# Attention feeding a mixture of experts: value products with the score tile stationary, and rows turned by DMA

## The chip, the cores and the metric

The kernel runs on one core of a Trainium2 chip. The metric is device time in microseconds (us), lower is better. The core has a matrix engine (TensorE, PE in the tables, with its weight loads as PEld), VectorE (DVE), ScalarE (ACT), GpSimd (POOL), and SyncE (SP), whose queue issues most DMAs. TensorE reads a stationary operand (loaded by LDWEIGHTS) and streams a moving one past it; results go to PSUM, eight banks of 128 x 512 f32.

## What is computed

```python
# u, v: (8, 2496, 256)   z: (8, 2496, 64)   w1: (8, 256, 1024)   w2: (8, 1024, 256)
scores = (1.0 / S) * z @ z.T                 # per batch, S = 2496
attn   = np.maximum(scores, 0.0) ** 2
x      = (u * (attn @ v)).reshape(B * S, D)  # D = 256
xn     = x / (norm(x) + 1e-6)                # rows
logits = xn @ en.T / tau                     # en: 8 normalized expert rows
e      = argmax(logits)                      # one expert per token
out    = softmax(logits)[e] * (relu(x @ w1[e]) @ w2[e])
```

All in f32 accuracy. The kernel gets it from f16 matmuls: an operand is scaled by a power of two and split into a high and a low f16 half, and a product is the sum of high x high, low x high and high x low.

## The kernel before

**Stages.** First attention for all 8 batches with routing of each finished group of tokens to a table of rows in DRAM (`xs`, sorted by expert), then the expert stage: slots of 256 or 128 rows of one expert, `slot_up` and `slot_down`.

**Attention.** A batch has 2496 tokens: 5 groups of query tokens (four of 512, the last of 448), and 20 tiles of 128 keys (the last of 64). A step is one key tile `s` against one group `g`, so 100 steps a batch, 800 in all. `scores` (two matmuls, L232 and L233) makes a tile of 128 keys x 512 tokens in PSUM, ScalarE applies relu and square (L235, L236), and `parts` splits it on VectorE into high and low half (`hl`, L242 and L243, five buffers). The score matrix is symmetric, so only 60 of the 100 steps of a batch compute their tile ("own" steps: `s // 4 >= g`); the other 40 read a tile that was turned by a DMA transpose (L250, tile `tt`) when its mirror was made. `LOOK = 3` makes scores three own steps ahead and halves two ahead.

**Value products.** `values` (L261 to L274) holds a 128 x 128 piece of v (`va` high, `vb` low) stationary and moves the score tile, 512 columns, past it. Its result is 128 columns of v by 512 tokens, two accumulators (`acc`, two of three PSUM banks of pool `psA`) for the 256 columns. In the last step of a group both halves of the 64 keys share a tile (`twin`), so it has four matmuls for six.

**Routing.** When a group is done, `route` returns a list of pieces; one is taken per step of the next group. `gate_x` (L302) multiplies by u, still with tokens along the columns. For each of the four blocks of 128 tokens, `turn` (L308, L309) multiplies the block in f32 by an identity with the expert rows beside it, which gives the rows by token and the logits in one PSUM bank (`pm`, one buffer), and `take` copies them out (L326 on ScalarE, L327 on VectorE). Then the norm (`root`, `scale`), the split of the row into f16 halves (L351, L352), the choice of the expert, its place by a small matmul (`rank`, L399, L400), and four indirect DMAs on POOL (L424) that write the rows (`row`, two buffers) to `xs`.

**Start and look-ahead.** v's scale needs its maximum. For every batch it is read once for that (`scan`, eight loads of 312 KB into two buffers, L104, L110) and once more tile by tile for the products (`vt`, L198). For the next batch, `ahead` spreads these pieces over the steps of the current one; weights of the experts are split along the way (`weights`).

**Order.** A scheduler places the instructions on each engine's queue; every engine then works through its queue in order.

## Time and profile before

| | |
|---|---|
| median of three runs | 2256.31 us (2252.34 to 2259.57) |
| the profiled execution | 2257.18 us |
| its span in the trace | 2255.4 us |
| PE busy | 2177.3 us, 97% |
| DVE busy | 1422.9 us, 63% |
| ACT busy | 1095.7 us, 49% |
| DMA queue 1 (SP), share of 16 engines | 50.8% |

A busy share says how long an engine had an instruction in it; ends of matmuls are modelled, so two starts in a row tell more than a length. A row of the waits says which engine waited for whom, in total, how often, and the longest.

### The profile page before, as it was taken

To read this page: it belongs to the slowest core of one execution; us is meant where nothing else is said; L and a number is where in the kernel's file an instruction comes from. 1 tells how busy PE (TensorE), PEld (TensorE's weight loads), DVE (VectorE), ACT (ScalarE), POOL (GpSimd) and SP (SyncE) were. 2 spreads that over 40 slices of the span, in tenths; PEclk is the share of its full clock that TensorE was granted. 3 is DMA by queue.
4 is the path that set the end of the run, shared out by engine and by line. 5 is a ranking of instruction groups with operands and counts; after the bars stand their busy time and mean duration, and the time that the engine had idled before them with its cause. 6 is when DMAs were issued, how large, how long until landed. Compare 5 with 4: busy or idle time off the path is not lost. (4 is left out here: it accounts for less than half of the span.)

```text
span 2255.4 us, 42995 instructions
## 1 busy us (share of the span) xinstructions
PE 2177.3 (97%) x14922; PEld 1430.6 (63%) x14922; DVE 1422.9 (63%) x4339; ACT 1095.7 (49%) x2201; POOL 354.2 (16%) x432
## 2 busy tenths in 40 slices
PE   6999999999999999999999999999999999999987
PEld 2444445445445444445445458888888888888886
DVE  7888879788788788888788655333333333333332
ACT  6667667667568577667666642222222222222221
POOL 0011111111111111111111112111111111111211
PEclk8999999999999999999999999999999999999998
DMA  7947766765947858776655535333123223167453
GB/s 186 231 105 211 166 165 145 190 148 136 229 102 192 190 118 199 155 181 144 155 140 112 101 93 147 74 86 94 48 72 109 48 74 107 51 181 218 120 137 108
DMA packets 528267, 308.30 MB, mean 137 GB/s; under 512 B 446885, under 2 KB 489390, under 8 KB 519856
## 3 DMA queue, kind: packets, MB, share of 16 engines
q1 hardware_dynamic: 512672, 264.31, 50.8%
q0 software_dynamic: 15376, 41.24, 5.0%
q8 instruction: 117, 1.92, 0.4%
q14 instruction: 102, 0.84, 0.1%
HBM read 287.91 MB, written 60.12 MB: 154 GB/s over the span
## 5 line engine op out<-in xcount | busy, mean ns | idle before, releaser
L235 ACT ACTIVATE a<-sc 128x512 f32<-128x512 f32 (+1 forms) x480 | 282.8, 589 | 169.7 <-PE sc L233 125.3
L236 ACT ACTIVATE a<-a 128x512 f32<-128x512 f32 (+1 forms) x480 | 299.8, 625 | 13.3
L836 POOL DMA_INDIRECT out_dram<-ot,me x163 | 158.6, 973 | 696.9 <-DVE ot L835 422.3
L274 PEld LDWEIGHTS <-vv 128*128 128x128 f16 x1520 | 149.0, 98 | 179.2 <-issue 8.8
L273 PEld LDWEIGHTS <-vv 128*128 128x128 f16 x1520 | 149.1, 98 | 173.6 <-issue 17.8
L272 PEld LDWEIGHTS <-vv 128*128 128x128 f16 x1520 | 149.0, 98 | 161.8 <-ACT vv L217 2.3
L424 POOL DMA_INDIRECT xs<-row,dsti x160 | 171.3, 1071 | 499.4 <-DMA xs<-row,dsti 336.3
L272 PE MATMUL acc<-tt,vv 128*128 128x512 f16 (+1 forms) x640 | 236.4, 369 | 9.4 <-DVE xt L302 9.3
L274 PE MATMUL acc<-tt,vv 128*128 128x512 f16 (+1 forms) x640 | 236.2, 369 | 0.0
L273 PE MATMUL acc<-tt,vv 128*128 128x512 f16 (+1 forms) x640 | 236.2, 369 | 0.0
L232 PE MATMUL sc<-z 128*128 128x512 f16 (+1 forms) x480 | 183.7, 383 | 10.7 <-DVE z L189 10.7
L233 PE MATMUL sc<-z,z 128*128 128x512 f16 (+1 forms) x480 | 183.8, 383 | 0.0
L829 PE MATMUL po<-w,hh 128*128 128x256 f16 x648 | 177.4, 274 | 3.1 <-DMA w<-wsd 3.1
L829 PE MATMUL po<-wb,hh 128*128 128x256 f16 x656 | 178.9, 273 | 0.0
L830 PE MATMUL po<-wb,hh 128*128 128x256 f16 x656 | 178.8, 273 | 0.0
L831 PE MATMUL po<-wb,hl 128*128 128x256 f16 x656 | 178.8, 273 | 0.0
L831 PE MATMUL po<-w,hl 128*128 128x256 f16 x648 | 177.4, 274 | 0.0
L830 PE MATMUL po<-w,hh 128*128 128x256 f16 x648 | 177.4, 274 | 0.0
L805 PEld LDWEIGHTS <-wa 128*128 128x128 f16 x1472 | 145.3, 99 | 30.2 <-DMA wa<-wsd 16.8
L806 PEld LDWEIGHTS <-wa 128*128 128x128 f16 x1472 | 145.4, 99 | 13.3
L807 PEld LDWEIGHTS <-wa 128*128 128x128 f16 x1472 | 145.4, 99 | 13.1
L835 DVE TENSOR_SCALAR ot<-po,me,w 128x256 f32<-128x256 f32 x81 | 40.8, 540 | 157.2 <-PE po L831 155.9
(4216 smaller groups left out, 5165.2 us busy)
## 6 DMA issues: line engine op xcount, KB each, us to landing
wa<-wsd SPq DMA_DIRECT2D x92, 1024.0 KB
wb<-wsd SPq DMA_DIRECT2D x46, 1026.0 KB
w<-wsd SPq DMA_DIRECT2D x46, 1026.0 KB
scan<-in_v_dram SPq DMA_DIRECT2D x64, 312.0 KB
vt<-in_v_dram SPq DMA_DIRECT2D x152, 128.0 KB
ut<-in_uT_dram SPq DMA_DIRECT2D x32, 512.0 KB
wr<-in_w_dram SPq DMA_DIRECT2D x16, 1024.0 KB
wsd<-wo SPq DMA_DIRECT2D x16, 1024.0 KB
```

What stands on the lines that cost most here:

```text
L232: nc.tensor.matmul(sc[:, :n], z1[:, ss], z1[:, t0:t0 + n], start=True, stop=False)
L233: nc.tensor.matmul(sc[:, :n], z1[:, ss], z2[:, t0:t0 + n], start=False, stop=True)
L235: state["at"] = nc.scalar.activation(a[:, :n], sc[:, :n], AF.Relu, scale=2.0 ** -SHIFT).ins
L236: nc.scalar.activation(a[:, :n], a[:, :n], AF.Square)
L272: nc.tensor.matmul(acc[k][:, :n], va, ph[:, :n], start=first, stop=False)
L273: nc.tensor.matmul(acc[k][:, :n], va, pl[:, :n], start=False, stop=False)
L274: nc.tensor.matmul(acc[k][:, :n], vb, ph[:, :n], start=False, stop=last)
L424: nc.gpsimd.indirect_dma_start(xs[:, :], bass.IndirectOffsetOnAxis(ap=loc["dsti"][:m, j:j + 1], axis=0), row[:m, j, :], None)
L829: nc.tensor.matmul(o, hh[:, f, t], wh, start=(f == 0), stop=False)
L830: nc.tensor.matmul(o, hh[:, f, t], wl, start=False, stop=False)
L831: nc.tensor.matmul(o, hl[:, f, t], wh, start=False, stop=(f == NF - 1))
L836: nc.gpsimd.indirect_dma_start(out, bass.IndirectOffsetOnAxis(ap=me.bitcast(U32)[:, j, 1:2], axis=0), ot[:, j, :], None, bounds_check=N - ...
```

## The change

Values: the stationary operand is a 128 x 128 piece of the score tile (128 keys by 128 tokens, one half), the moving operand is v's high or low half, 256 columns; an accumulator bank holds two blocks of 128 tokens by 256 columns. A pair of banks holds the group's four blocks. In the 448-token group, the 64 odd tokens' high and low halves stand side by side (`apart`, `both`), so one load serves both. Turned tiles of that group are laid out to match, and the last key tile is turned in two DMAs.

Routing: `gate_x` writes rows by token at once; `turn` and the old `take` are gone. ScalarE makes the high half of the row (it was VectorE's), `flips` turns the f16 row by four DMA transposes on SP's queue, and three empty pieces later `logits` multiplies the turned halves by the split expert rows (`enr`), 16 small matmuls for a group, which one `take` reads. `row` has three buffers; u is read by token and its tile has one buffer; PSUM: three banks for scores, four for accumulators.

Start and look-ahead: the first batch's v is loaded once in five loads, kept in buffers of the turned tiles, and reduced there; for later batches the scan pieces begin at step 4 and stand four steps apart, each reduction eight steps after its load.

```diff
-    psS = ctx.enter_context(tc.tile_pool(name="psS", bufs=4, space=PSUM))
-    psA = ctx.enter_context(tc.tile_pool(name="psA", bufs=3, space=PSUM))
+    psS = ctx.enter_context(tc.tile_pool(name="psS", bufs=3, space=PSUM))
+    psA = ctx.enter_context(tc.tile_pool(name="psA", bufs=4, space=PSUM))
...
+    def first_load(c0):
+        if c0 % VB == 0:
+            first[c0 // VB] = tp.tile([P, VB, D], F32, name="vall", tag="tt")
+        t = first[c0 // VB]
+        j = c0 % VB
+        m = min(VC, NST - c0)
+        full = min(m, S // P - c0)
+        if full:
+            nc.sync.dma_start(t[:, j:j + full, :], v[0, c0 * P:(c0 + full) * P, :].rearrange("(j p) d -> p j d", p=P))
...
         n = groups[g][1]
-        vv = Vs[b, s]
-        first, last = s == 0, s == NST - 1
-        for k in ks:
-            va = vv[:, k * P:(k + 1) * P]
-            vb = vv[:, D + k * P:D + (k + 1) * P]
+        va, vb = Vs[b, s][:, 0:D], Vs[b, s][:, D:]
+        last = s == NST - 1
+        for j in range(ceil_div(n, P)):
+            m = min(P, n - j * P)
+            o = acc[j // 2][:, (j % 2) * D:(j % 2 + 1) * D]
+            first = s == 0 and j % 2 == 0
+            ph, pl, both = hl(j)
             if twin and last:
-                nc.tensor.matmul(acc[k][:, :n], va, ph[:, :n], start=first, stop=False)
-                nc.tensor.matmul(acc[k][:, :n], vb, pl[:, :n], start=False, stop=True)
-                continue
-            nc.tensor.matmul(acc[k][:, :n], va, ph[:, :n], start=first, stop=False)
-            nc.tensor.matmul(acc[k][:, :n], va, pl[:, :n], start=False, stop=False)
-            nc.tensor.matmul(acc[k][:, :n], vb, ph[:, :n], start=False, stop=last)
+                todo = [(o[:m], ph, va), (o[:m], pl, vb)]
+            elif both is not None:
+
+                todo = [(o, both, va), (o[:m], ph, vb)]
+            else:
+                todo = [(o[:m], ph, va), (o[:m], ph, vb), (o[:m], pl, va)]
+            for k, (dst, w, x) in enumerate(todo):
+                nc.tensor.matmul(dst, w, x, start=first and k == 0, stop=last and k == len(todo) - 1,
+                                 skip_group_check=True)
...
-        row = rt.tile([P, 4, ROW], F32, name="row", tag="row")
+        row = rt.tile([P, 4, ROW], F32, name="row", tag="row", bufs=3)
...
         def gate_x():
             for k in range(2):
-                nc.vector.tensor_tensor(xt[:, k, :n], acc[k][:, :n], ut[:, k, :n], op=ALU.mult)
-
-        def turn(j):
-            def f():
-                pm = psM.tile([P, 512], F32, name="pm", tag="m")
-                c = slice(j * P, (j + 1) * P)
-                nc.tensor.matmul(pm[:, 0:P + E], xt[:, 0, c], rhs0, start=True, stop=False, skip_group_check=True)
-                nc.tensor.matmul(pm[:, P:2 * P + E], xt[:, 1, c], rhs1, start=False, stop=True, skip_group_check=True)
-                loc["pm"] = pm
-                state["pm"] = True
-                if j:
-                    square(j - 1)
-            return f
+                m = min(2, full - 2 * k)
+                if m > 0:
+                    nc.vector.tensor_tensor(x[:, 2 * k:2 * k + m, :], acc[k].rearrange("p (j d) -> p j d", d=D)[:, :m, :],
+                                            ut[:, 2 * k:2 * k + m, :], op=ALU.mult)
+            if rem:
+                o = acc[full // 2][:, (full % 2) * D:(full % 2 + 1) * D]
+                if apart(g):
+                    t = rt.tile([P, D], F32, name="tl", tag="sq", bufs=1)
+                    nc.scalar.copy(t[:rem], o[rem:])
+                    nc.vector.tensor_tensor(t[:rem], o[:rem], t[:rem], op=ALU.add)
+                    o = t
+                nc.vector.tensor_tensor(x[:rem, full, :], o[:rem], ut[:rem, full, :], op=ALU.mult)
...
         def split(j):
             up = loc["up"][:, j:j + 1]
-            nc.vector.tensor_scalar_mul(row16[:, j, 0:D], x[:, j, :], up)
+            nc.scalar.activation(row16[:, j, 0:D], x[:, j, :], AF.Copy, scale=up)
             nc.vector.scalar_tensor_tensor(row16[:, j, D:2 * D], x[:, j, :], up, row16[:, j, 0:D],
                                            op0=ALU.mult, op1=ALU.subtract)
 
@@ -357,6 +432,32 @@
                 for j in range(j0, min(j0 + 2, nj)):
                     split(j)
             return f
+
+        def flips(j0):
+
+            def f():
+                for j in range(j0, min(j0 + 2, nj)):
+                    nc.sync.dma_start_transpose(xt[:, j], row16[:, j, 0:2 * D])
+            return f
+
+        def logits():
+            pm = psM.tile([P, 512], F32, name="pm", tag="m")
+            for j in range(nj):
+                for c in range(4):
+                    w = 2 * E if c < 2 else E
+                    nc.tensor.matmul(pm[:, 2 * E * j:2 * E * j + w], xt[:, j, c, :], enr[:, c % 2, 0:w],
+                                     start=(j == 0 and c == 0), stop=(j == nj - 1 and c == 3), skip_group_check=True)
+            loc["pm"] = pm
+            state["pm"] = True
+
+        def take():
+            pv = loc.pop("pm")[:, 0:2 * E * nj].rearrange("p (j a e) -> p j a e", a=2, e=E)
+            state["pm"] = False
+            lo = rt.tile([P, 4, E], F32, name="lo", tag="lo")
+            nc.vector.tensor_copy(lo[:, :nj, :], pv[:, :, 1, :])
+            nc.vector.tensor_tensor(lg[:, :nj, :], pv[:, :, 0, :], lo[:, :nj, :], op=ALU.add)
+            nc.vector.tensor_tensor(lg[:, :nj, :], lg[:, :nj, :],
+                                    loc["inv"][:, :nj].unsqueeze(2).broadcast_to([P, nj, E]), op=ALU.mult)
...
+        wait = lambda: None
+        return [gate_x, squares(0), squares(2), root, scale, splits(0), splits(2), flips(0), flips(2), wait, wait, wait,
+                logits, take, top, exps, rank, gates, place, scatters]
...
@@ -870,15 +964,15 @@
     def ahead(b):
 
         todo = []
-        at = min(NST + 4, NB // 4)
+        at = min(4, NB // 16)
         for i, what in enumerate(SCANS):
-            todo.append((at + 2 * i, False, lambda w=what: scan_load(b + 1, *w)))
-            todo.append((at + 2 * i + 4, False, lambda w=what: scan_max(b + 1, *w)))
-        at += 2 * len(SCANS) + 4
+            todo.append((at + 4 * i, False, lambda w=what: scan_load(b + 1, *w)))
+            todo.append((at + 4 * i + 8, False, lambda w=what: scan_max(b + 1, *w)))
+        at += 4 * len(SCANS) + 8
         for k, what in enumerate("zv"):
             for j, f in enumerate(scale_pieces(b + 1, what)):
-                todo.append((at + 8 * k + 4 * j, True, f))
```

What the scheduler makes of it shows at three places. TensorE, in the second group of the second batch, where the first group is being routed (`acc` are accumulators, `tt` and `hl` score tiles, `vv` v's halves, `pm` the routing bank). Before:

```order
L274 LDWEIGHTS vv
L274 MATMUL acc_2901<-tt,vv 128x512
L308 MATMUL pm<-rhs_234,xt 128x136
L309 MATMUL pm<-rhs_235,xt 128x136
L232 LDWEIGHTS z_322
L232 MATMUL sc<-z_322 128x512
L233 LDWEIGHTS z_322
L233 MATMUL sc<-z_323,z_322 128x512
L272 LDWEIGHTS vv
L272 MATMUL acc_2900<-hl__2873,vv 128x512
```

and now:

```order
L350 LDWEIGHTS hl__3831
L350 MATMUL acc_3583<-vv,hl__3831 128x256
L448 LDWEIGHTS xt
L448 MATMUL pm<-enr,xt 128x16
L448 LDWEIGHTS xt
L448 MATMUL pm<-enr,xt 128x16
L448 LDWEIGHTS xt
L448 MATMUL pm<-enr,xt 128x8
L448 LDWEIGHTS xt
L448 MATMUL pm<-enr,xt 128x8
```

The two f32 matmuls of a turn, which stood at four places of a group, are gone; 16 small ones (four of them here) stand at one place; and a value matmul loads a score tile and moves 256 columns of `vv`.

SP's queue, from the end of the first group of the second batch into the second (`ut` is u, `scan` a piece for the maximum of the next batch, `xt` the turned row). Before:

```order
L250 DMA_TRANSPOSE tt<-hl__2798 128x8x128
L250 DMA_TRANSPOSE tt<-hl__2820 128x8x128
L250 DMA_TRANSPOSE tt<-hl__2843 128x8x64
L281 DMA ut<-in_uT_dram 128x2x512
L250 DMA_TRANSPOSE tt<-hl__2997 128x8x128
L104 DMA scan<-in_v_dram 128x624
L250 DMA_TRANSPOSE tt<-hl__3019 128x8x128
L250 DMA_TRANSPOSE tt<-hl__3041 128x8x128
L104 DMA scan<-in_v_dram 128x624
L250 DMA_TRANSPOSE tt<-hl__3059 128x8x128
```

and now:

```order
L295 DMA_TRANSPOSE tt<-hl__3492 128x8x128
L292 DMA_TRANSPOSE tt<-hl__3528 128x4x64 x2
L105 DMA scan<-in_v_dram 128x624
L359 DMA ut<-in_u_dram 128x4x256
L105 DMA scan<-in_v_dram 128x624
L440 DMA_TRANSPOSE xt<-row 128x4x128 x4
L295 DMA_TRANSPOSE tt<-hl__3759 128x8x128
L105 DMA scan<-in_v_dram 128x624
L295 DMA_TRANSPOSE tt<-hl__3784 128x8x128
L295 DMA_TRANSPOSE tt<-hl__3809 128x8x128
```

The four flips stand in front of the second group's first turns of score tiles, behind the load of u.

VectorE at the start, around the reductions for v's maximum (`smxv`, now `smxf`; `z` are split z tiles). Before:

```order
L589 TENSOR_SCALAR eh<-en2c 8x1
L188 SCALAR_TENSOR_TENSOR z_104<-zt,scz,z_103 64x256
L591 TENSOR_SCALAR ey<-eh 8x1
L189 SCALAR_TENSOR_TENSOR z_103<-zt,scz,z_104 64x256
L594 TENSOR_TENSOR et<-ey 8x1
L242 CAST hl__377<-a 128x512
L596 SCALAR_TENSOR_TENSOR et_263<-et,en2c 8x1
L392 TENSOR_SCALAR row<-iot 128x4
L243 TENSOR_TENSOR hl__377<-a,hl__377 128x512
L110 TENSOR_REDUCE smxv<-scan 128x1
L598 SCALAR_TENSOR_TENSOR ey<-et_263,ey 8x1
L122 TENSOR_REDUCE smv<-smxv 128x1
```

and now:

```order
L234 TENSOR_REDUCE smxf<-vall 128x1 x2
L189 SCALAR_TENSOR_TENSOR z_104<-zt,scz,z_103 64x256
L276 CAST hl__174<-a 128x512
L234 TENSOR_REDUCE smxf<-vall 128x1
L284 TENSOR_TENSOR hl__174<-a,hl__174 128x512
L276 CAST hl__177<-a 128x512
L234 TENSOR_REDUCE smxf<-vall 128x1
L284 TENSOR_TENSOR hl__177<-a,hl__177 128x512
L190 SCALAR_TENSOR_TENSOR z_103<-zt,scz,z_104 64x256
L123 TENSOR_REDUCE smv<-smxf 128x1
```

The last of the reductions stands 27 places further ahead in VectorE's queue than it did.

## Rows read from the trace of the kernel before

**Rows 1.** the page, busy time of each engine, share of the span:

```profile
PE 2177.3 (97%) x14922; PEld 1430.6 (63%) x14922; DVE 1422.9 (63%) x4339; ACT 1095.7 (49%) x2201; POOL 354.2 (16%) x432
```

**Rows 2.** stretches: us, busy of each engine, clock, DMA share, GB/s:

```profile
10.00:15.00 5.00, 3.22 (x8) 1.27 (x9) 4.77 (x10) 3.15 (x7) 0.00 (x0) 1.00 0.74 226
199.53:235.74 36.21, 36.21 (x181) 17.80 (x180) 29.95 (x95) 27.68 (x54) 4.55 (x6) 1.00 0.76 143
304.94:341.38 36.44, 33.77 (x162) 16.49 (x162) 27.53 (x95) 22.61 (x52) 4.53 (x7) 0.95 0.70 190
704.54:740.04 35.50, 35.50 (x178) 17.50 (x177) 30.91 (x97) 28.87 (x58) 5.16 (x6) 1.00 0.97 218
1600.00:1800.00 200.00, 200.00 (x1835) 179.25 (x1833) 71.47 (x114) 45.38 (x76) 36.96 (x38) 1.00 0.28 73
```

**Rows 3.** TensorE in order of time: start, modelled length, line, matmul:

```profile
711.29 0.40 PE L308 MATMUL pm<-rhs,xt 128*128 128x136 f32 x2
...
711.75 0.38 PE L232 MATMUL sc<-z 128*128 128x512 f16 x1
...
715.20 0.40 PE L308 MATMUL pm<-rhs,xt 128*128 128x136 f32 x2
...
1360.27 0.27 PE L805 MATMUL ph__17140<-xt,wa 128*128 128x256 f16 x1
```

**Rows 4.** the page, costliest groups: a weight load of the value products:

```profile
L274 PEld LDWEIGHTS <-vv 128*128 128x128 f16 x1520 | 149.0, 98 | 179.2 <-issue 8.8
```

**Rows 5.** waits of TensorE, 70 to 1360 us: total, times, longest:

```profile
PE acc L272 <- DVE xt L302: 9.3, 14, 1.6
PE pm L308 <- DVE lg L327: 8.4, 10, 2.2
```

**Rows 6.** the page, costliest groups: a matmul of the down projection:

```profile
L830 PE MATMUL po<-wb,hh 128*128 128x256 f16 x656 | 178.8, 273 | 0.0
```

**Rows 7.** TensorE in order of time: rank matmuls, and 128 columns:

```profile
99.05 0.26 PE L399 MATMUL pm<-ob,ones_b 128*128 128x40 bf16 x4
...
99.18 0.38 PE L232 MATMUL sc<-z 128*128 128x512 f16 x1
...
2150.41 0.22 PE L805 MATMUL ph__30475<-xt,wa 128*128 128x128 f16 x1
2150.47 0.22 PE L806 MATMUL ph__30475<-xt,wa 128*128 128x128 f16 x1
```

**Rows 8.** VectorE, then TensorE in order of time, around a late row:

```profile
326.93 0.17 DVE L392 TENSOR_SCALAR row<-iot 128x4 int32<-128x4 f32 x1 [4.30 <-DMA xs<-row,dsti]
...
330.23 0.38 PE L272 MATMUL acc<-hl__4009,vv 128*128 128x512 f16 x1 [1.81 <-DVE hl__4009 L242]
```

**Rows 9.** VectorE and ScalarE by line, 300 to 1300 us: busy, mean ns:

```profile
L352 DVE SCALAR_TENSOR_TENSOR row<-x,up,row 128x256 f16<-128x256 f32 x120 | 56.9, 475 | 0.0
L351 DVE TENSOR_SCALAR row<-x,up 128x256 f16<-128x256 f32 x120 | 41.1, 345 | 0.0
L327 DVE COPY lg<-pm 128x8 f32<-128x8 f32 x120 | 19.4, 161 | 72.5 <-ACT x L326 72.1
...
L217 ACT ACTIVATE vv<-vt,scv 128x256 f16<-128x256 f32 x114 | 55.2, 502 | 16.3 <-PE acc L274 13.3 <-issue 0.9 <-DMA vt<-in_v_dram 0.7
L326 ACT COPY x<-pm 128x256 f32<-128x256 f32 x120 | 43.9, 366 | 114.9 <-PE pm L309 107.8 <-issue 7.0
```

**Rows 10.** a turn on SP (ns); DMA queue 1 from 208 to 232:

```profile
L250 SPq DMA_TRANSPOSE tt<-hl__2524 x1: 1237/1237/1237, 206.7 to 206.7; - x1
...
q1 hardware_dynamic: 13097, 3.26, 79.8%
```

**Rows 11.** the start: VectorE, TensorE in order of time; a ScalarE wait:

```profile
25.54 0.78 DVE L110 TENSOR_REDUCE smxv<-scan 128x1 f32<-128x624 f32 x1
...
30.32 0.63 PE L272 MATMUL acc<-hl__191,vv 128*128 128x512 f16 x1
...
ACT vv L217 <- DMA vt<-in_v_dram: 3.0, 4, 1.2
```

155 lines of the change are left out of this document (95 added, 60 removed).

## The prediction

> **What bounds the kernel now.** I read the busy table first: TensorE is busy 97% of the span, the next engine 63% [rows 1]. A busy TensorE is modelled, so I then read starts. In the table by stretches, attention (as 704 to 740) and experts (1600 to 1800) both run at a granted clock of 1.00 [rows 2]. In attention every matmul of 512 columns starts 0.2156 us after the one before: 16 from 711.75 to 715.20 [rows 3]; for 448 columns I take 0.189, in proportion. So attention is a chain of matmuls on TensorE, and the reader can add it up from counts. A batch has 100 steps, each with six value matmuls (four in the last step of a group; 4560 of the loads are on three lines with x1520 [rows 4]). That is 3776 value matmuls of 512 columns and 944 of 448: 3776 x 0.2156 + 944 x 0.189 = 992.5 us. The 60 own steps of a batch have two score matmuls each, 56 x 16 x 0.2156 + 4 x 16 x 0.189 = 205, unchanged. The expert stage, from 1360.27 on [rows 3], is unchanged too.
>
> What is not arithmetic in attention is small: waits. The list of waits from 70 to 1360 names two at its head: the accumulators wait for the gating product L302 (14 times, 9.3 us), and a turn matmul L308 waits for the logits copy L327 (10 times, 8.4 us) [rows 5].
>
> **The change, part by part.**
>
> *Value products.* The stationary operand becomes a 128x128 piece of the score tile and the moving one v's 256 columns. A full step has 12 matmuls of 256 columns for six of 512, so the columns stay; the count doubles. In the last group of a batch (448 tokens) a step has 9 + 2, because the 64 odd tokens share one load for high and low half. Total 32 x (19 x 12 + 8) + 8 x (19 x 11 + 8) = 9288. What one costs with a load of its own shows in the expert stage, where both projections move 256 columns [rows 6]: 1835 matmuls and 1833 loads in 200 us, 0.109 apart [rows 2]. 9288 x 0.109 = 1012.4, so **+19.9 us**. A load is 98 ns long [rows 4] and lies under the matmul before it; the cover is 109 ns, so it is nearly used up.
> The Trainium skill ("TensorE: Matmul & The Clock Gate", Part 3, The mechanism) says that a weight load overlaps running matmuls only when it goes to another row group. Here all use the whole array. By that rule the trace's down projection could not run at 0.109; it does. What the rule would give is a rival below.
>
> *Turns.* Rows by token need no turning, so 160 pairs of f32 matmuls go. A pair takes 711.29 to 711.75, 0.46 us [rows 3]: **-73.6 us**, all on TensorE.
>
> *Logits.* 16 small matmuls for each of 40 groups, each with its own load of 128 columns. No row shows 8 or 16 columns. Nearest are the rank matmuls, 40 columns with a load each: five between 99.05 and 99.18, 0.025 apart [rows 7]; the other end is 128 columns at 0.056 [rows 7]. I take the rank rows, which are nearer: 640 x 0.025 = **+16.0** (up to 35.8).
>
> *Waits that lose their cause.* With four accumulator banks for two groups, the next group no longer waits for L302; with one read of the logits bank per group instead of four, the waits at L308 go. Their listed 17.7 us count from a modelled end, 0.38 after a start where the spacing is 0.216, so each of 24 hides 0.16 more: **-21.5**. The third row buffer takes away a stall that starts on VectorE: at 326.93 it had stood 4.30 us for the scatter that frees a row, and TensorE then waited 1.81 (with the hidden part 2.0) for a score tile [rows 8]. Its group, 305 to 341, ran at a mean clock of 0.95 [rows 2], 1.8 of 36.4 us lost. Together **-3.8**. Of the four score banks one goes to the accumulators: nothing, since a score tile is read by ScalarE three steps before its bank is needed again.
>
> *Waits that may come.* VectorE loses the scaling L351 and the copies L327 (41.1 and 19.4 us in 300 to 1300 [rows 9]) and gets two small reads of the logits bank per group; ScalarE loses the copy L326 (43.9) and gets the scaling, by the nearest row L217 0.50 each, 60 us for the same 120 [rows 9]. Neither becomes the bound. u's tile has one buffer now, so its load waits for the gating product on SP, in front of the flips, which need that product anyway: nothing. The rows are now turned by DMA, four per group, on SP's queue. A turn of a score tile costs SP 1.24 us to issue [rows 10]; for half the bytes I take the same, since no row is smaller. Four cost 4.9 us per group, and the odd 64 tokens split one turn into two. Queued behind them on SP are the turns of the score tiles, and for those waits VectorE, which needs one of five score buffers back. On the DMA engines, 208 to 232 is nearly all such turns: 3.26 MB at 79.8%, 170 GB/s [rows 10], so a flip of 131 KB is 0.77 us, 3.1 per group. The first group of a batch, 199.53 to 235.74, stands at 0.76 (27.5 of 36.2 us [rows 2]) and would hold, with flips and four scans moved into it (312 KB at 226 GB/s over a share of 0.74, 1.0 us each [rows 2]), about 35 of 35 us. That is full; but 704 to 740 ran at 0.97 with TensorE without a gap [rows 2]. The logits stand four steps (5 us or more) behind the last flip, which covers the landing in most groups. Bounds 0 and 40 us; I take **+8**, near the row at 0.97.
> The Trainium skill ("Advanced Engine Details and Errata", X-Bar Transpose (TRN2)) calls such turns as fast as ordinary DMA, 350 to 400 GB/s. The row says 170; by the page a flip would be 0.35 us (an estimate) and this overload would not exist.
>
> *Start.* v's maximum is read with two buffers, so eight loads follow VectorE's pace, the last reduction starts at 25.54 and the first value matmul at 30.32 [rows 11]. Now five loads go out at once behind the first z loads, and stay for the products. 2.56 MB at 226 GB/s [rows 2] is 11.3 us, less than half of the time to the last reduction, so data comes several us earlier; but VectorE is busy 4.77 of 5 us there [rows 2] and its work before the first split is nearly the same. After it, ScalarE waited 3.0 us for v tiles in the first group [rows 11]; those are now there. Between 0 and 12; I take **-7**.
>
> **Sum**, against the profiled execution's 2257.2 (span 2255.4, 1.8 outside; 0.9 over the median of the three runs): +19.9 - 73.6 + 16.0 - 21.5 - 3.8 + 8 - 7 = -62.0, that is 2195.2, or **2195 us**.
>
> **Rivals.**
> *Only the arithmetic comes.* The waits are replaced by as many at the flips or in the full first groups, logits cost 0.056, the start gives nothing: 2257.2 + 19.9 - 73.6 + 35.8 = 2239. For it: the schedule before was planned as well and still had these waits; the DMA share. Against: fewer hand-overs between engines per group. 2215 to 2245.
> *Slower: SP's queue.* In the first two groups of a batch SP reaches the first flip before the split row is written and stands there; score turns queue behind it, the five buffers run out, VectorE's next cast waits and TensorE with it. Price per group: about 24 small VectorE steps of 0.16 (as L327) and four splits of 0.475 [rows 9], 5.7 us, plus 4.9 us of issue, less three buffers at 1.74 us a step (2 x 0.2156 + 12 x 0.109): 5.4. Sixteen groups: 86 us, 2281. It decides when SP comes more than about 5 us early; over 4.3 us a group (69 in all) the kernel is slower than before. Against: in the new order on SP the flips stand behind a load that waits for the gating product, so they come late rather than early.
> *Loads not hidden* (the page's rule): every load adds its 98 ns, 4568 more of them: 448 us, about 2643. The down projection speaks against it.
> *More goes.* From 30.32 to 1360.27 pass 1330 us; the arithmetic above with turns and small matmuls is about 1276, so 54 are waits of every kind, of which I took 25. If the start gives 12, nothing new comes and the other 29 go as well: 2195 - 5 - 8 - 29 = 2153; 2153 to 2175. Against: some of the 29 are the scale and weight pieces, which stay.
>
> **How the numbers follow.** Forecast 0.62 (2175 to 2215), arithmetic only 0.20, more 0.09, SP's queue 0.06, loads not hidden 0.01, no change 0.02. Range 2170 to 2240: it takes in the forecast, most of the next case and some of the better one. A measurement of this kernel can tell about 0.3% from no change; faster by more 0.91, within 0.02, slower 0.07.
>
> **What would show it.** Right: value matmuls 0.109 apart, expert stage at the same length, attention ending near 1299 instead of 1360, no wait of accumulators for the gating product, logits 0.025 apart, first value matmul near 26. Wrong: spacing above 0.11 (loads); TensorE waiting at the logits for DMA or at score tiles in first groups (SP, DMA); a first value matmul still near 30.

## The result: slower by 0.7%, and the profile after

The changed kernel takes 2271.5 us (median of 7 runs, 2265.9 to 2272.5); the kernel before, beside it, 2254.0. The ratio is 1.0071, 95% interval 1.0056 to 1.0087. The forecast was 2195. The profiled execution has a span of 2269.6 us where that of before had 2255.4: +14.2 in place of -62.0, 76 us off. The busy table, as in [rows 1]:

```profile
PE 2175.7 (96%) x19490; PEld 1797.7 (79%) x19490; DVE 1416.3 (62%) x4143; ACT 1101.0 (49%) x2209; POOL 361.1 (16%) x432
```

TensorE is still the busy one. I split its span by the starts of its matmuls, as the prediction did. I call "attention" the time from the first value matmul to the first expert matmul, and a group's stretch runs from its first value matmul to that of the next group.

| | before | after | forecast for after |
|---|---|---|---|
| first value matmul, us | 30.3 | 24.1 | 23.3 |
| attention, us | 1329.9 | 1340.7 | 1275 |
| first expert matmul to the end, us | 895.1 | 904.8 | 895 |

(The forecast for the first row takes all of the -7 of the start as coming ahead of the first value matmul. The prediction itself named one "near 26", which leaves some of the 7 to the first group.)

So 66 of the 76 us are in attention and 10 in the expert stage. To see what they are I took every start-to-start time in attention above the plain spacing of its kind (0.2156 for 512 columns, 0.189 for 448, 0.109 for 256, the median for small ones). Before, this excess is about 51 us (the prediction had 54). After, it is about 97, where the sum allowed some 30.

The list of waits of TensorE in attention, as [rows 5] (total, times, longest):

```profile
PE pm L448 <- DMA xt<-row: 7.2, 10, 1.8
PE pm L500 <- DVE ob L478: 6.1, 3, 2.8
PE pm L561 <- DVE lg L458: 5.1, 4, 2.0
PE sc L266 <- ACT a L269: 2.4, 2, 2.2
```

The two waits that stood at the head before are gone, as forecast: no accumulator waits for the gating product. In their place stand the logits waiting for a turned row, and the rank matmul L500 waiting for VectorE's one-hot tile.

Stretches (engines' busy time, clock, DMA share, GB/s), as in [rows 2]: the last group of the second batch, first in the kernel before and then, in the rows that follow, in the changed one; there also the first group of the third batch, the last group of the last batch, the start of the expert stage, and its middle:

```profile
340.68:367.47 26.79, 26.64 (x150) 14.71 (x149) 24.00 (x87) 19.74 (x47) 5.44 (x9) 1.00 0.55 153
328.29:362.35 34.06, 31.18 (x251) 21.33 (x249) 25.35 (x86) 19.63 (x46) 5.87 (x9) 1.00 0.58 140
362.35:400.23 37.88, 35.16 (x297) 27.13 (x296) 31.43 (x98) 27.05 (x54) 4.51 (x6) 1.00 0.90 165
1335.77:1364.83 29.06, 29.06 (x242) 20.40 (x240) 10.93 (x51) 5.57 (x16) 3.17 (x5) 1.00 0.69 185
1364.80:1500.00 135.20, 121.43 (x1085) 106.45 (x1085) 55.57 (x171) 32.12 (x62) 27.31 (x29) 0.95 0.33 86
1600.00:1800.00 200.00, 200.00 (x1835) 179.25 (x1833) 71.55 (x115) 45.92 (x77) 37.89 (x39) 1.00 0.29 73
```

The middle of the expert stage is as before. The last group of the second batch took 26.8 us in the kernel before and takes 34.1 here; in the first seven batches these groups took 26.8 to 30.6 and take 30.8 to 35.6. In the last batch, which has no next batch to load, it takes 29.1 (24.7 before). That difference is the thread to follow.

Two things show in single rows. First, a shape of matmul that I had not priced. TensorE in order of time, in the last group of the first batch (start, modelled length; a row's count includes the matmuls that follow it in the answer):

```profile
168.97 0.50 PE L350 MATMUL acc<-vv,tt 128*128 128x256 f16 x2
169.17 0.51 PE L350 MATMUL acc<-vv,tt 128*64 128x256 f16 x2
169.40 0.39 PE L350 MATMUL acc<-vv,tt 128*128 128x256 f16 x2
```

The matmul at 169.17 has 64 stationary columns: the 64 odd tokens. It starts 0.202 after the one ahead, the next 0.230 after it, and the one after that 0.120 later: 0.552 where three of the plain ones take 0.327. There are 152 such places and 8 with two in a row, about 37 us.

Second, SP, ScalarE, VectorE and TensorE in the last group of the second batch:

```profile
338.66 2.53 SPq L440 DMA_TRANSPOSE xt<-row  x2
341.28 1.93 SPq L199 DMA_DIRECT2D vt<-in_v_dram  x1
343.30 2.50 SPq L440 DMA_TRANSPOSE xt<-row  x2
345.89 1.00 SPq L199 DMA_DIRECT2D vt<-in_v_dram  x2
...
344.93 0.51 ACT L251 ACTIVATE vv<-vt,scv 128x256 f16<-128x256 f32 x1 [1.79 <-DMA vt<-in_v_dram]
348.25 0.51 ACT L251 ACTIVATE vv<-vt,scv 128x256 f16<-128x256 f32 x1 [2.81 <-DMA vt<-in_v_dram]
352.74 0.50 ACT L247 ACTIVATE vh<-vt,scv 64x256 f16<-64x256 f32 x1 [3.98 <-DMA vt<-in_v_dram]
...
353.81 0.48 DVE L252 SCALAR_TENSOR_TENSOR vv<-vt,scv,vv 128x256 f16<-128x256 f32 x1 [3.31 <-ACT vv L251]
...
354.73 0.27 PE L500 MATMUL pm<-ob,ones_b 128*128 128x40 bf16 x4 [1.79 <-DVE ob L478]
```

Read it downwards. The flips (L440) and the next batch's loads of v (L199) share SP's queue, and between 338.66 and 346.9 SP issues four flips and no more than three loads of v. So v tiles come late; ScalarE, in order, waits for them three times; VectorE waits for ScalarE; and the one-hot tile for the rank matmul, which has nothing to do with v, stands behind that in VectorE's order. TensorE then waits at L500. Over attention ScalarE waits 25.0 us for v tiles at L251 and 24.3 at L247 (before: 8.0 in all), and SP stands at a flip for about 170 us in all, most of it for VectorE, at the head of the list for the split row:

```profile
ACT vv L251 <- DMA vt<-in_v_dram: 25.0, 12, 3.4
ACT vh L247 <- DMA vt<-in_v_dram: 24.3, 7, 5.1
...
SPq L440 <- DVE row L427: 44.9, 20, 6.0
```

At the start of the expert stage the last flips and what is queued behind them show directly, 13.8 us where before had 3.5 there:

```profile
PE po L923 <- DMA wb<-wsd: 6.1, 1, 6.1
PE pm L448 <- DMA xt<-row: 5.5, 4, 2.4
PE ph__22237 L899 <- DMA wa<-wsd: 2.2, 1, 2.2
```

### The profile page after: what moved, and what is told of

Read it like the earlier page. It is cut to its first block, busy times and chain, and to the rows that moved or that the text cites. A ratio compares the mean times of both kernels' runs of the same rounds, so it can differ in the third digit from the quotient of the medians.

```text
span 2269.6 us, 52531 instructions
## 1 busy us (share of the span) xinstructions
PE 2175.7 (96%) x19490; PEld 1797.7 (79%) x19490; DVE 1416.3 (62%) x4143; ACT 1101.0 (49%) x2209; POOL 361.1 (16%) x432
## 5 line engine op out<-in xcount | busy, mean ns | idle before, releaser
L350 PE MATMUL acc<-vv,tt 128*128 128x256 f16 (+1 forms) x3712 | 442.8, 275 | 0.0
L350 PEld LDWEIGHTS <-tt 128*128 128x128 f16 (+1 forms) x3712 | 355.1, 98 | 80.0 <-issue 28.2
L525 POOL DMA_INDIRECT xs<-row,dsti x160 | 181.7, 1136 | 490.2 <-DMA xs<-row,dsti 357.1
L924 PEld LDWEIGHTS <-hh 128*128 128x128 f16 x1304 | 128.1, 98 | 22.9 <-issue 7.9
L929 DVE TENSOR_SCALAR ot<-po,me,wb 128x256 f32<-128x256 f32 x82 | 41.3, 540 | 159.2 <-PE po L925 159.2
L925 PEld LDWEIGHTS <-hl 128*128 128x128 f16 x1304 | 128.1, 98 | 15.4
L923 PEld LDWEIGHTS <-hh 128*128 128x128 f16 x1304 | 128.1, 98 | 15.0
```

What stands on the lines that cost most here:

```text
L350: nc.tensor.matmul(dst, w, x, start=first and k == 0, stop=last and k == len(todo) - 1, skip_group_check=True)
L525: nc.gpsimd.indirect_dma_start(xs[:, :], bass.IndirectOffsetOnAxis(ap=loc["dsti"][:m, j:j + 1], axis=0), row[:m, j, :], None)
L923: nc.tensor.matmul(o, hh[:, f, t], wh, start=(f == 0), stop=False)
L924: nc.tensor.matmul(o, hh[:, f, t], wl, start=False, stop=False)
L925: nc.tensor.matmul(o, hl[:, f, t], wh, start=False, stop=(f == NF - 1))
```

## Experiments

Lines in these kernels differ from the changed kernel's by a few. Times are medians; the kernel before, run beside each, took 2250.6 to 2252.7. Attention is that of the one profiled execution, which lay up to 4 us off the median, in e14 5 and in e6 6 us under it; differences in attention of a few us mean little. Where the logits are taken of a constant tile, all tokens choose alike and the expert stage is shorter, so those kernels are compared in attention, and in total only with each other.

| run | time, us | ratio to before | attention, us |
|---|---|---|---|
| e1_wide | 2267.0 | 1.0062 [1.0043, 1.0081] | 1341.7 |
| e2_no_flips * | 2188.5 | 0.9722 [0.9705, 0.9740] | 1278.2 |
| e9_cols_no_flips * | 2202.4 | 0.9771 [0.9749, 0.9794] | 1300.4 |
| e5_idle_flips * | 2259.0 | 1.0040 [1.0024, 1.0055] | 1338.5 |
| e6_loads_on_act | 2267.0 | 1.0083 [1.0067, 1.0098] | 1326.3 |
| e12_idle_loads_act * | 2227.1 | 0.9885 [0.9862, 0.9908] | 1302.1 |
| e13_free_flips * | 2355.7 | 1.0467 [1.0446, 1.0489] | 1435.1 |
| e18_quarter_flips * | 2220.2 | 0.9863 [0.9846, 0.9879] | 1301.7 |
| e3_old_ahead | 2262.1 | 1.0050 [1.0031, 1.0069] | 1329.0 |
| e4_flips_on_act | 2365.5 | 1.0507 [1.0489, 1.0526] | 1435.7 |
| e7_loads_on_pool | 2299.9 | 1.0213 [1.0197, 1.0229] | 1372.3 |
| e8_rows_on_pe | 2263.2 | 1.0047 [1.0034, 1.0061] | 1335.2 |
| e10_logits_later | 2267.5 | 1.0055 [1.0034, 1.0076] | 1336.1 |
| e11_later_v_pairs | 2259.5 | 1.0028 [1.0015, 1.0042] | 1326.8 |
| e14_all_later_act | 2251.2 | 0.9999 [0.9983, 1.0014] | 1315.8 |
| e15_all_old_ahead | 2270.6 | 1.0078 [1.0055, 1.0102] | 1339.1 |
| e17_mixed_rows | 2255.3 | 1.0011 [1.0001, 1.0022] | 1324.6 |
| e16_two_rows | 2345.5 | 1.0411 [1.0384, 1.0439] | 1412.6 |

(* logits of a constant tile.)

### The shape and the flips: a square of four kernels

Without the matmuls of 64 stationary columns:

```
-            if twin and last:
-                todo = [(o[:m], ph, va), (o[:m], pl, vb)]
-            elif both is not None:
-                todo = [(o, both, va), (o[:m], ph, vb)]
+            if both is not None:
+                todo = [(o, both, va)] if twin and last else [(o, both, va), (o, both, vb)]
+            elif twin and last:
+                todo = [(o[:m], ph, va), (o[:m], pl, vb)]
```

> Edit to the changed kernel: the 64 odd tokens of a batch's last group use the load of 128 columns (high and low half side by side) for the low half of v too, and in the step of 64 source tokens for the only product, so that no matmul with 64 stationary columns is left (the low times low product comes in, the output keeps its meaning). Theory A, the change of shape costs: in the changed kernel's trace a matmul of 256 columns with 64 stationary columns between such of 128 took 0.202 up to its start, 0.229 after it and 0.120 after the next, 0.551 in place of 0.327; 160 such places, and 8 with two in a row, are about 37 us, which go: 2271.5 - 37 = 2234, ratio to the kernel before about 0.991, last groups of a batch 4.5 us shorter. Rival B, the last groups wait for data anyway (rows turned by DMA, v tiles): the 37 us turn into waits in the same groups and the time falls by 10 or less, to 2260 or more.

Without the flips as well:

```
-        xt = rt.tile([P, 4, 4, P], F16, name="xt", tag="xt", bufs=1)
+        xt = state["xt0"]
...
-                for j in range(j0, min(j0 + 2, nj)):
-                    nc.sync.dma_start_transpose(xt[:, j], row16[:, j, 0:2 * D])
+                pass
```

> As e1_wide, and the turns of the rows by DMA are left out: the logits are taken of a constant tile (their values are meaningless and so is the choice of experts; the number of matmuls, the scatters and everything else stays). Theory A, the flips are what brought the new waits in attention (on SP's queue in front of v loads, score turns and weight loads, or as DMA traffic): against e1_wide the waits at the logits (7.2 us listed in attention, 5.5 at the start of the experts), the wait for weights there (6.1) and most of the waits of TensorE for VectorE at the rank matmuls and score tiles go, 20 to 30 us in all: ratio to e1_wide 0.987 to 0.991. Rival B, the waits come from the new order of scans and reductions in the first groups or from the splits on ScalarE: only the waits at the logits and at the first experts go, 8 to 14 us, ratio 0.994 to 0.996.

With the 64-column matmuls, without the flips (the second edit alone):

> The changed kernel with its matmuls of 64 stationary columns (as it was put on record), and the flips left out as in e2_no_flips (logits of a constant tile, their values are meaningless). The fourth corner of a square: with both 2271.5, without the 64-column matmuls 2267.0, without both 2188.5. Theory A, each costs its time and in the last groups of a batch the longer of the two holds: without flips the 64-column matmuls cost their 37 us in full, 2188 + 30 to 37 = 2218 to 2226, last groups 4.5 us longer than in e2_no_flips. Rival B, the 64-column matmuls hide under other work whatever the flips do: 2188 to 2200.

The 37 us of the shape stand in the trace, and taking them away brings 4.5 us: rival B. The last groups of seven batches stay nearly as long as they were, 230.6 us together for 236.2; only the last batch's falls by the price of the shape, from 29.1 to 24.8. Without flips the last group of the second batch is 26 us, and the first group behind it 36.0 in place of 40.1. First e1_wide (last group of the second batch, first group of the third, last group of all), then e2_no_flips, the same three:

```profile
333.30:365.73 32.43, 28.52 (x249) 23.49 (x247) 24.59 (x85) 19.25 (x46) 6.35 (x9) 0.95 0.57 145
365.73:405.78 40.05, 36.84 (x297) 27.81 (x296) 31.84 (x99) 27.26 (x55) 4.24 (x6) 0.96 0.84 155
1341.38:1366.16 24.78, 24.64 (x242) 21.92 (x239) 10.64 (x52) 5.57 (x16) 3.27 (x5) 1.00 0.66 196
```

```profile
321.40:347.80 26.40, 26.38 (x249) 22.53 (x247) 24.22 (x85) 19.20 (x46) 5.51 (x9) 1.00 0.51 142
347.80:383.81 36.01, 35.02 (x298) 27.17 (x297) 31.89 (x99) 27.27 (x55) 4.96 (x6) 1.00 0.84 160
1278.02:1302.51 24.49, 24.49 (x242) 21.87 (x240) 10.62 (x51) 5.57 (x16) 3.36 (x5) 1.00 0.68 198
```

With the odd shape mended the flips cost 64 us of attention (1341.7 against 1278.2): theory A of e2, and more than twice its 20 to 30 us. By the medians of the times, less the 21.6 us by which the expert stage is shorter in e2's trace, it is 57. In the changed kernel itself, with the shape in it, they cost 40 (1340.7 against 1300.4 in e9). The engines' order does not explain it: with the flips left out, VectorE and ScalarE have the same order in attention in both kernels, and SP's differs by six places at most. ScalarE's waits for v tiles, 57 us in e1_wide, are 24 without the flips. With the flips gone the shape costs 14 us of time and 22 of attention, between the two expectations and nearer to B: part of its 37 us covers waits that a last group has even without flips. So the two do not add up. Each holds the last groups by itself, and the flips hold them longer.

Where the 64 us lie: 34 in the last groups of the first seven batches, 25 in the first and second groups, 4 in the third.

What they are made of shows in TensorE's clock. The stretch of attention in e1_wide, the same in e2_no_flips, and two score matmuls of e1_wide behind the rank matmul at 357.45, for which TensorE had stood 2.33 us:

```profile
24.41:1366.16 1341.75, 1282.75 (x11112) 1034.38 (x11111) 1077.13 (x3501) 887.29 (x1844) 192.95 (x250) 0.98 0.77 171
24.31:1302.51 1278.20, 1255.92 (x11112) 1025.30 (x11112) 1075.35 (x3501) 889.71 (x1844) 195.01 (x250) 1.00 0.71 164
357.45 0.27 PE L499 MATMUL pm<-ob,ones_b 128*128 128x40 bf16 x4 [2.33 <-DVE ob L477]
359.97 0.63 PE L266 MATMUL sc<-z 128*128 128x512 f16 x1
360.39 0.63 PE L267 MATMUL sc<-z,z 128*128 128x512 f16 x1
```

The two score matmuls start 0.42 apart, where 0.2156 is usual: the lower of the clock's two levels. In attention of e1_wide the clock fell to it only behind stands of TensorE such as this one. Matmuls at that level take about 21 us more than their plain spacing in e1_wide, 5 in the changed kernel and 2 in e2_no_flips. So of the 64 us some 19 are matmuls at the lower level and some 44 are waits. It also shows where the gain of e1 went: without the odd shape TensorE waits 20 us more than in the changed kernel, as rival B has it, and loses another 16 to the clock. All six executions of e1_wide had a granted clock of 0.981 to 0.985 over the whole kernel, all seven of the changed kernel 0.986 to 0.993.

Attention without both, 1278.2, is 3 us above the forecast's 1275; but that holds +8 for the flips, so the rest of the sum was 11 us short in all. u's single buffer and the three score banks, both put at nothing, are in e2_no_flips too, so what they cost is within these 11.

### How the flips cost: what waits for them, or what stands behind them

The logits read a constant tile but the flips stay (e5); the next batch's loads go to ScalarE's queue (e6); both (e12):

```
-                    nc.tensor.matmul(pm[:, 2 * E * j:2 * E * j + w], xt[:, j, c, :], ...
+                    nc.tensor.matmul(pm[:, 2 * E * j:2 * E * j + w], state["xt0"], ...
```

```
-        nc.sync.dma_start(vt[:n], v[b, s * P:s * P + n, :])
+        (nc.sync if b == 0 else nc.scalar).dma_start(vt[:n], v[b, s * P:s * P + n, :])
```

(the second in the same way for the other loads of v and z)

> As e1_wide, with the flips issued on SP from the same rows and at the same places, but the logits taken of a constant tile (their values are meaningless, as in e2_no_flips): SP's queue and the DMA engines carry all that they did, and TensorE waits for no flip. In e1_wide attention (first value matmul to first expert matmul) is 1342 us, in e2_no_flips 1278. Theory A, SP's queue: what stands behind the flips (loads of v and z, turns of score tiles) is late and the logits are only one of several that wait: attention 1315 to 1335, time 2225 to 2245. Rival B, the latency of a flip in the chain from row to logits: attention 1278 to 1292, time 2188 to 2202.

> As e1_wide, with the loads of z and v for the next batch (36 in the last group of a batch and the end of the one before) issued on ScalarE's DMA queue in place of SP's; same traffic. Of e1_wide the last batch, which has no such loads, has groups of 36.7, 31.2, 31.5, 28.9 and 23.0 us, as e2_no_flips has without flips (35.4, 32.5, 30.9, 29.5, 22.7), while the last groups of the other batches take 31 to 35. Theory A, SP's queue is full in those groups (flips 5 us and loads 15 to 17 in line): without the loads they fall to 26 to 28, seven times 5 to 7 us, 35 to 45 in all, 2222 to 2232. Rival B, ScalarE's share of the issue (0.5 us each) and its waits make the splits late: no gain over 10 us, or slower.

> e5_idle_flips and e6_loads_on_act in one: flips issued on SP that nothing waits for (logits of a constant tile, values meaningless), the next batch's loads of z and v on ScalarE's queue. Attention was 1342 us in e1_wide, 1339 in e5_idle_flips, 1327 in e6_loads_on_act, 1278 in e2_no_flips. Theory A, the two effects of a flip (loads behind it on SP, logits behind its landing) stand beside each other and each alone is enough to hold the group: with both taken away attention is near that without flips, 1280 to 1295, time 2190 to 2210. Rival B, a third effect (the flips' traffic on the DMA engines, or ScalarE's issue of the loads) holds it: 1305 or more.

Taking away only the wait at the logits gives 3 us of attention, on the side of theory A of e5 and even above its 1315 to 1335: the wait moves on to the rank matmul, because VectorE is late by the v tiles. Taking the loads off SP gives 15 us of attention in the profiled execution, which was the fastest of its four, but nothing in the median: in time rival B of e6, though not for its reason, since now the logits themselves wait. The heads of the two lists of waits, e5 and then e6:

```profile
PE pm L499 <- DVE ob L477: 34.6, 6, 7.3
```

```profile
PE pm L447 <- DMA xt<-row: 28.6, 26, 2.3
```

With both taken away, last groups are down (27.70 in the second batch, the row below) and attention is 1302.1, between what A and B asked and nearer to B. So in last groups two effects stand beside each other, loads behind the flips and logits behind their landing, each enough to hold the group. Of the 64 us these give back 40, of which 28 lie in the last groups of the first seven batches.

```profile
322.85:350.55 27.70, 26.38 (x249) 22.55 (x247) 26.09 (x88) 20.59 (x48) 5.04 (x8) 1.00 0.57 151
```

Of the other 24, some 18 are in first and second groups, where SP carries the turns of the score tiles, and 6 in last groups. Some of the groups in which e12 loses have full DMA engines, as this first group of the fifth batch (36.2 us in e2_no_flips):

```profile
680.50:720.01 39.51, 36.18 (x296) 26.52 (x295) 31.22 (x93) 28.67 (x59) 4.15 (x6) 1.00 1.03 221
```

That could be traffic or the queue. Two runs were made to part them. In e13 the flips turned a constant tile:

> As e12_idle_loads_act, and the flips turn a constant tile, so that on SP none of them ever waits for a row; their number, bytes and places in SP's order stay (values meaningless as before). In e12_idle_loads_act attention is 1302 us, 24 above e2_no_flips, most of it in the first and second group of a batch, where VectorE stands for a score buffer whose turn is late. Theory A, SP stands at a flip whose row is not written, and the score turns behind it are late: attention 1278 to 1290, time 2203 to 2215. Rival B, the issue time of the flips or their traffic is enough: attention 1297 to 1305, time 2222 to 2230.

It took 2355.7 us and does not part the two: with no row to wait for, the order on SP was built with all flips but the last group's moved ahead, into the first 393 us. There SP's queue held everything up (groups of 44 to 65 us from the second on, up to 413). Behind that no flip is left until the last group, and the groups that were dearest in e12 are as short as without flips: the second of the fourth batch 33.2 (e12 40.6, e2 33.4), the first of the fifth 35.4 (39.5 and 36.2). So it is the flips that hold them, not ScalarE's issue of the loads, which e13 has as well. A kernel that cuts a dependency has to be read in its order before its time.

In e18 each flip of e12 turns a quarter of its bytes, in nearly the same order on SP:

```
-                    nc.sync.dma_start_transpose(xt[:, j], row16[:, j, 0:2 * D])
+                    nc.sync.dma_start_transpose(xt[:, j, 0], row16[:, j, 0:P])
```

> As e12_idle_loads_act, and each flip turns 128 of the row's 512 columns only, a quarter of the bytes (nothing reads the result, values meaningless); the flips stay in number, in their places on SP, and wait for the same rows. In e12_idle_loads_act attention is 1302 us, 24 above e2_no_flips, most of it in first and second groups, in the worst of which the DMA engines are busy 1.00 to 1.04 of the time. Theory A, SP's queue (standing for a row, and the issue time, if it does not fall with the bytes): attention 1297 to 1305, time 2222 to 2230. Rival B, the traffic of the flips: attention 1278 to 1290, time 2203 to 2215. If the issue of a flip falls well under 1.24 us, the run cannot part the two.

Attention is 1301.7, the same as e12's 1302.1: the queue, not the traffic. SP's time for a flip did not fall with the bytes (median 1.18 us, in e12 1.22), and the rows show the first score turn of the group behind four of them:

```profile
561.89 5.20 SPq L439 DMA_TRANSPOSE xt<-row  x4
567.18 1.26 SPq L295 DMA_TRANSPOSE tt<-hl__9242  x1
```

How these 24 us divide between SP standing for an unwritten row and SP issuing stays open.

### Other queues, other places

> As e1_wide, with the turns of the rows issued on ScalarE's DMA queue in place of SP's; the DMA traffic is the same. Theory A, what costs is SP's queue (loads of v, turns of score tiles and weight stores behind a flip that waits for its row): ScalarE's waits for v tiles (49 us listed in the changed kernel, before 5) and the waits of TensorE behind them go, less 5 us of issue a group on ScalarE, which has room outside first groups: 8 to 15 us faster than e1_wide. Rival B, what costs is the traffic: the waits at the logits and for v tiles stay, ScalarE's issue delays score tiles, and the time is 0 to 30 us above e1_wide.

> As e1_wide, with the loads of z and v for the next batch issued on GpSimd's DMA queue. Theory A, as in e6_loads_on_act, with GpSimd 16% busy: 2222 to 2235. Rival B, GpSimd stands at each scatter for the one before (490 us of waits listed in the changed kernel), four in a row, so v tiles come later than from SP: 2270 or more.

> As e1_wide, with the due times of the next batch's scans, maxima, scale pieces and z loads as in the kernel before (scans from the second group on). Theory A, the scans and maxima in the first group of a batch are what makes it long (VectorE and the DMA engines are fullest there): first groups fall from 36.4 to 40.2 us to about 35 to 37, some 2 us each in seven batches, 10 to 15 us, ratio to e1_wide 0.993 to 0.996. Rival B, the first groups are long because of weight pieces and waits on SP and ScalarE, and the scans only move the load: no difference within 5 us, or slower by 5 to 10, because the z loads and v loads come together in the last group.

Flips on ScalarE's queue cost 98 us more than on SP (e4, rival B and beyond it): ScalarE stands for the row with score tiles behind it (TensorE's listed wait for a score tile is 24.5 us, in the changed kernel 2.4), and the first groups of the later batches take 43 to 49 us. Loads on GpSimd cost 33 us more (e7, rival B). The old due times for scans gain 5 us (e3, rival B), within what two intervals of 0.2% can tell; first groups fall by 0 to 3 us, and last groups stay at 31 to 35.

### The third row buffer

```
-        row = rt.tile([P, 4, ROW], F32, name="row", tag="row", bufs=3)
+        row = rt.tile([P, 4, ROW], F32, name="row", tag="row")
```

> As e1_wide, with two row buffers in place of three, as in the kernel before. Theory A, the third buffer takes away a stall where VectorE waits for a scatter to free a row (4.3 us once in the kernel before, 9.1 in all): 2 to 10 us above e1_wide, a wait of VectorE for the scatter of 4 us or more in its trace. Rival B, in the new order the rows are freed in time: within 3 us of e1_wide and no such wait.

Theory A in kind, but 78 us where it said 2 to 10: VectorE waits 105.9 us for a scatter to free a row, before 9.1. A row's buffer is now also read by the flips, and GpSimd's write into it (L493) waits 272.7 us for them. With three buffers that write waits nearly as long, 226.8 us in the same stretch of e1_wide; what the third takes away is VectorE's wait:

```profile
DVE row L492 <- DMA xs<-row,dsti: 105.9, 22, 8.0
...
POOL row L493 <- DMA xt<-row: 272.7, 30, 78.7
```

### Can the gain be kept

e8 turns the rows on TensorE again, as fp16; e10 moves the logits further behind the flips; e11 loads v two tiles at a time; e14 joins e10, e11 and e6; e15 adds the old due times; e17 turns the rows of the last groups on TensorE and the others by DMA. The edits of e8 and e10:

```
+                for c in range(4):
+                    nc.tensor.matmul(pm[:, c * P:(c + 1) * P], row16[:, j, c * P:(c + 1) * P], state["id16"], ...
...
+            nc.vector.tensor_copy(xt[:, j], pm)
```

```
-        return [gate_x, squares(0), squares(2), root, scale, splits(0), splits(2), flips(0), flips(2), wait, wait, wait,
-                logits, take, top, exps, rank, gates, place, scatters]
+        return [gate_x, both(squares(0), squares(2)), both(root, scale), splits(0), splits(2), flips(0), flips(2),
+                wait, wait, wait, wait, wait, logits, both(take, top), exps, wait, rank, gates, place, scatters]
```

> As e1_wide, with the rows turned on TensorE: per 128 tokens four matmuls of fp16, 128 columns each with its own load, against a unit matrix, and one copy by VectorE; no flips on SP. 640 x 0.056 = 36 us on TensorE, and a copy of 512 columns, 160 in all. Theory A (the flips are the cause of the lost time, attention 1278 without them): attention 1278 + 36 and 0 to 15 of waits for copies, 1314 to 1329, and the start of the experts as in the kernel before; 2230 to 2250, at or under the kernel before. Rival B, the turns wait for VectorE's splits and copies as the kernel before's did, or VectorE is late by the 60 us that the copies add: 2260 or more.

> As e1_wide, with the same steps put otherwise in the queue behind a group: squares in one step, root and scale in one, so that the flips come two steps earlier, and five empty steps in place of three ahead of the logits. In e1_wide TensorE stands 23 us more than the matmuls need at the logits, in the last groups above all. Theory A, the chain from row to logits (four issues of 1.24, landing 3 to 5) is longer than its three steps of 1.2 us: the waits at the logits go, 15 to 25 us less, 2242 to 2252. Rival B, as e5_idle_flips showed, the wait moves to the rank matmul because VectorE is late there by the v tiles: 0 to 8 us less, 2259 or more.

> As e10_logits_later, and the tiles of v for the next batch are loaded two at a time, in as many bytes: ten loads fewer on SP in the last group of a batch, each about 0.5 us. Theory A, SP's issue is what makes the v tiles late: 5 us of 32 less on SP, ScalarE's waits for v tiles (25 and 24 us listed in the changed kernel) fall to under 20, 10 to 20 us less than e10_logits_later, 2225 to 2242. Rival B, the loads are late because SP stands at flips whose rows are not written yet, however many loads there are: within 5 us of e10_logits_later.

> As e11_later_v_pairs, with the next batch's loads of z and v on ScalarE's queue as in e6_loads_on_act; its output keeps its meaning. Theory A, the two effects of the flips in last groups are now both eased (fewer and moved loads, five empty steps ahead of the logits), first groups stay as they are: attention 1305 to 1315, time 2232 to 2246, under the kernel before. Rival B, ScalarE's issue of the loads holds up its splits of the rows, the logits wait again: attention 1325 or more, 2255 or more.

> As e14_all_later_act, with the due times of scans, maxima and z loads as in the kernel before (as in e3_old_ahead, which was 5 us under e1_wide). Theory A, first groups lose scans and their maxima and so some 1 to 2 us each in five batches: 5 to 10 us under e14. Rival B, the z loads come together with the flips of the last group and cost as much there: within 4 us of e14 or above it.

> As e14_all_later_act, and the rows that are turned during the last group of a batch, and those of the very last group, are turned on TensorE as in e8_rows_on_pe (eight groups of 40; 16 matmuls of 128 columns and four copies by VectorE each); all others by DMA. Theory A, in last groups the chain through the flips is what still holds e14 (24 us of waits at the logits, 32 in all last groups), and the start of the experts waits for the last flips: 15 to 25 us of attention go, less 8 x 0.9 us for the matmuls, and up to 8 at the start of the experts: 2224 to 2242, under the kernel before. Rival B, VectorE's copies (0.6 us each) come into groups in which it is nearly full, so waits at the turns take the place: 2246 or more.

e10 gains nothing (rival B), as e5 foretold; e11 8 us, between the two, and ScalarE's waits for v tiles fall from 58.9 only to 51.1; e14, which eases both effects, 16 us against e1_wide. That brings it level with the kernel before, though not under it: between the two expectations, nearer to A. e15 is worse (rival B). e8 and e17 show rival B too. Rows on TensorE need VectorE and ScalarE at once, and the turns wait for the copy (e8, first row) or for the split (e17, second row):

```profile
PE pm L439 <- DVE xt L449: 16.9, 19, 1.9
```

```profile
PE pm L444 <- ACT row L430: 12.4, 6, 3.0
```

No version that takes its logits from the rows was faster than the kernel before. In last groups VectorE is busy for 24 to 25 us of what would be 26; I take it that any step of the row's chain that needs it then comes late, which no run shows by itself.

## Why the prediction was wrong, step by step

- **Value products, +19.9.** The spacing of 0.109 with a load each is right. Wrong is that all 9288 were priced as one shape: 168 of them have 64 stationary columns and cost about 37 us more in spacing, 22 of attention when the flips are left out (e9 against e2). The trace of before could only hint at it. There L134, whose stationary operand has one row (1*128), starts 0.31 after a score matmul whose spacing is 0.216; but L124, whose stationary operand has one column (128*1), starts on time:

```profile
291.03 0.38 PE L233 MATMUL sc<-z,z 128*128 128x512 f16 x1
291.34 0.27 PE L134 MATMUL pm<-smbz,ones_f 1*128 1x1 f32 x1
...
285.74 0.38 PE L233 MATMUL sc<-z,z 128*128 128x512 f16 x1
285.96 0.27 PE L124 MATMUL pm<-idt,smz 128*1 128x128 f32 x1
```

- **Turns, -73.6.** Right: they are gone.
- **Logits, +16.0.** Right in size: 0.025 apart at the median. Another 9.4 us at them is waiting, which belongs to the flips.
- **Waits that lose their cause, -21.5.** Those waits are gone. The third row buffer, -3.8, was priced by the stall it removes, not by the need the change makes for it: without it the new order loses 78 us.
- **Waits that may come, +8 (0 to 40).** This is the step that failed: the flips cost 40 us of attention in the changed kernel and 64 with the odd shape mended. The issue time of 1.24 us [rows 10] was right. But I sized the term by the DMA share of a first group, and gave every group "four steps (5 us or more)" of cover at the logits. In last groups a step is 1.2 us (11 x 0.109), and on SP stand the next batch's loads. I listed the score turns as what is queued behind a flip, and left out the loads of z and v, which stand there as well. Nor did I count what TensorE loses at the lower level of its clock, some 19 of the 64 us.
- **Start, -7.** Right: 6.2.
- **Expert stage, unchanged.** Its middle is. Its start is not: the last flips and the weight loads behind them are waited for, most of the 9.7 us.

Of the rivals, SP's queue (2281, chance 0.06) names the cause, with TensorE's cost in the wrong place: I put it into the first two groups, where it is the smaller part (25 of 64). That 2281 lies near the measured 2271.5 is partly luck; the price also keeps the +8 beside it, which the rival's own threshold of 69 us leaves out (2273 without). The argument against it, that the flips come late rather than early, fails: SP stood about 170 us at flips.

In `after` itself the parts are 37 us of shape, about 60 of waits and clock against about 30 in the sum, and 10 in the expert stage: 37 + 30 + 10 = 77 for the 76. This is bookkeeping of one trace. The square shows that the first two are not independent: without the shape, waits and clock rise to 98.

## What to carry to other kernels

When work moves from a compute engine to a DMA queue, add up that queue group by group, with the loads that already stand in it, and follow what each late load holds up in the in-order engines. A stage with short steps is where a fixed latency shows first, so check the shortest steps, not the busiest group. And read which shapes the trace does not hold: 168 matmuls of an odd shape cost as much spacing here as 340 of the common one.

## What the runs showed of the hardware that was not expected

- A matmul of 256 columns with 64 stationary columns among such of 128 costs 0.22 us over its plain 0.109. With two in a row, the second starts 0.133 after the first: entering and leaving the shape is most of the price.
- SP took 5.20 us for four turns of 128x128 (e18, above) and 5.49 for four of 128x512 at the same place of e12; the median of one is 1.18 and 1.22. Its issue time does not follow the bytes.
- The granted clock is 0.95 in the last group of e1_wide above, where TensorE stood 2.33 us at a rank matmul, and 1.00 in the same group without flips, and in that of the changed kernel, where the same wait was 1.79: a wait can cost more than its length. Behind it two 512-column matmuls start 0.42 apart, where 0.2156 is usual: the lower of the clock's two levels, 1.2 in place of 2.4 GHz. Over attention this made some 21 us in e1_wide.
